# Strassen's scheme for the first feed-forward product of three quarters of an attention, mixing and feed-forward kernel

## The chip, the core and the metric

One core of one Trainium2 chip runs the whole program in one launch. The metric is the device time of the launch in microseconds; lower is better. The engines are TensorE (PE, with its weight loads as PEld), VectorE (DVE), ScalarE (ACT), GpSimd (POOL) and the DMA queues, of which SyncE (SP) issues nearly all. Each engine works through its own list of instructions in order and waits for the others by semaphores.

## What is computed

Three stages follow each other; all arrays are float32 at the end, the large weights arrive as float64 (two 32-bit words each).

```python
# attention, 2 x 8 heads, 768 positions, 64 wide: a local band and 24 block sums
scores_l = scale * q @ k.T           # kept where |i - j| < 16
scores_s = scale * q @ k_sum.T + log(32)
a = softmax(concat([scores_l, scores_s]));  attn = a @ concat([v, v_sum])
# first mixing block, x = attn as (2, 768, 512)
u = x + (x.T @ U @ V).T
x2 = u + relu(u @ w_ch1) @ w_ch2     # w_ch1 512 x 2048, w_ch2 2048 x 512
# second mixing block
xk = mu_k * x2 + (1 - mu_k) * x2_prev;  xr = mu_r * x2 + (1 - mu_r) * x2_prev
out = sigmoid(xr @ w_r) * (relu(xk @ w_k)**2 @ w_v)   # w_k 512 x 1024, w_v 1024 x 512
```

## The kernel before

Every large product is made of three: a number is split into a high part (a copy rounded to the type that TensorE takes, `fp32r`) and a low part (the rest), and high x high, high x low and low x high are added up in PSUM. The high part is made on ACT (`relu_high` L600, `block` L556, `split_high` L739), the low part on DVE or POOL (`relu_low` L605, `block` L560, `split_low` L742, `mix_low` L698).

The order of everything is written out by hand as two lists of steps, `ORDER` (attention, and the first quarter of the feed-forward block for batch 0) and `ORDER2` (the rest). A step is a name and its indices, and calls one function, which issues a few instructions on one or two engines. The list fixes the order on every engine, the SP queue among them.

Of `ORDER2`, in the order of time:

- The feed-forward block. The 2048 hidden columns are four quarters `q` of 512; batch `b` has 768 positions, in two halves `c` of 384. For each (q, b, c) and each of four tiles `i` of 128 hidden columns, `f1` (step `fa`, L595) makes 12 matmuls 128x128 by 128x384 into a bank, `relu_high` (`fh`) and `relu_low` (`fl`) make the two parts of the hidden tile from the bank, and `f2` (`fb`, L618) makes 12 matmuls into four accumulating banks. After four tiles `y_sum` (`fy`, L626) adds the four banks to `y` on DVE. The list alternates `fa` of the next tile with `fb` of this one. `y_rest` (`yr`, L491) adds the low part of `u` to `y` on POOL.
- Weights: 54 blocks of 128x512 float64 are loaded (`cl`) and converted by hand: two ACT steps (`ca` L512, `cb` L515), three DVE steps on SBUF (`cc` L519, `cs` L525, `cg` L529), one POOL addition (`cp` L541); then, for the blocks of `w1`, `w2` and `wr`, the high part on ACT (`ch` L556) and the low part on POOL (`co` L560). They come in the order w1/w2 by quarters, wk, wr, wv; those of wk and wv stay in SBUF (`quads`).
- The product with w_r (`ra`, L707), then `k = xk @ w_k` and the product with w_v, both by Strassen's scheme: seven products (`ka` L772, `va` L804) of sums of quadrants instead of eight of the quadrants. The sums of weights, of `xk` and of the squared hidden values are made by `sums` (L736; `wks`, `xs`, `wvs`, `ms`, with a `p` behind the name on POOL, without it on DVE), split by L739 and L742, and the products are combined from PSUM on DVE (`k_take` L778, `v_take` L816).

`take` and `give` hand out the eight banks of PSUM in turn; SBUF regions are shared by hand (`SLOTS`, `PLACE`).

## Time and profile before

| | us |
|---|---|
| median of 3 runs (498.65 to 501.3) | 500.97 |
| profiled execution | 499.92 |
| its span, first to last instruction | 498.1 |
| PE busy | 484.7 (97%) |
| DVE busy | 401.4 (81%) |
| ACT busy | 276.2 (55%) |
| POOL busy | 252.3 (51%) |

Busy time is the union of an engine's instructions. The span is read in stages: attention and the first half of quarter 0 up to 107.5 us, the second half of quarter 0 up to 141, quarters 1 to 3 up to 341.9, the products with w_r and w_k up to 434, the product with w_v and the output up to 498.1. A row of the view of stages has the engine's busy time in that stage and, in brackets, its instructions. A row of instructions has line, engine, operation, output from input by tile names, shapes, the count, the busy time in us, the mean of one in ns, and the idle time before them with what ended it. Instructions of DVE overlap by some tens of ns, so busy time is a little under the sum of the single ones.

### The profile page before, as it was taken

To read this page: it belongs to the slowest core of one execution; us is meant where nothing else is said; L and a number is where in the kernel's file an instruction comes from. 1 tells how busy PE (TensorE), PEld (TensorE's weight loads), DVE (VectorE), ACT (ScalarE), POOL (GpSimd) and SP (SyncE) were. 2 spreads that over 40 slices of the span, in tenths; PEclk is the share of its full clock that TensorE was granted. 3 is DMA by queue.
4 is the path that set the end of the run, shared out by engine and by line. 5 is a ranking of instruction groups with operands and counts; after the bars stand their busy time and mean duration, and the time that the engine had idled before them with its cause. 6 is when DMAs were issued, how large, how long until landed. Compare 5 with 4: busy or idle time off the path is not lost.

```text
span 498.1 us, 9378 instructions
## 1 busy us (share of the span) xinstructions
PE 484.7 (97%) x3636; PEld 464.1 (93%) x3636; DVE 401.4 (81%) x790; ACT 276.2 (55%) x532; POOL 252.3 (51%) x203
## 2 busy tenths in 40 slices
...
GB/s 312 320 255 216 230 186 50 100 0 170 128 126 138 116 128 168 144 145 135 102 111 1 0 1 1 2 1 84 86 1 1 0 1 1 1 5 60 1 22 169
DMA packets 18061, 46.34 MB, mean 93 GB/s; under 512 B 2897, under 2 KB 7377, under 8 KB 18017
## 3 DMA queue, kind: packets, MB, share of 16 engines
...
q10 hardware_dynamic: 144, 0.18, 0.1%
...
q0 software_dynamic: 32, 0.05, 0.0%
...
## 4 chain that ended last, share of the span: by engine, by line
PE 79%; DVE 10%; ACT 6%; DMA 3%; issue 1%; SPq 0%; DVEq 0%
PE bank L595 24%; PE bank L618 23%; PE bank L772 7%; PE bank L707 7%; PE bank L640 4%; PE bank L663 4%; DMA vt<-vt 3%; PE bank L370 2%; PE bank L415 2%; DVE U L742 2%; PE bank L399 2%; PE bank L804 2%; PE bank L467 1%; DVE N L742 1%; DVE V L742 1%; PE bank L437 1%
## 5 line engine op out<-in xcount | busy, mean ns | idle before, releaser
L541 POOL TENSOR_TENSOR A<-C,A 128x512 int32<-128x512 int32 (+1 forms) x38 | 52.6, 1386 | 50.2 <-DVE C L525 45.0
L605 DVE SCALAR_TENSOR_TENSOR h<-bank,h 128x384 fp32r<-128x384 f32 x56 | 30.9, 552 | 45.0 <-ACT h L600 44.7
L600 ACT ACTIVATE h<-bank 128x384 fp32r<-128x384 f32 x56 | 27.4, 488 | 68.1 <-PE bank L595 68.1
L529 DVE SCALAR_TENSOR_TENSOR A<-stg,A 128x512 int32<-128x512 int32 (+1 forms) x54 | 54.0, 1004 | 6.9 <-ACT A L512 4.8
L512 ACT ACTIVATE A<-stg 128x512 f32<-128x512 uint32 (+1 forms) x54 | 36.4, 673 | 35.5 <-DMA stg<-w 18.6
L519 DVE TENSOR_SCALAR C<-C 128x512 f32<-128x512 f32 (+1 forms) x54 | 43.7, 810 | 3.3 <-POOL A L541 2.0
L525 DVE TENSOR_SCALAR C<-C 128x512 int32<-128x512 int32 (+1 forms) x54 | 41.6, 773 | 0.8
L515 ACT ACTIVATE C<-stg 128x512 f32<-128x512 f32 (+1 forms) x54 | 36.2, 673 | 7.6 <-POOL N L541 5.6
L804 PE MATMUL bank<-N,U 128*128 128x256 f32 x252 | 35.9, 280 | 0.5 <-DVE E L816 0.5
L618 PE MATMUL bank<-h,D 128*128 128x384 f32 x192 | 35.9, 336 | 0.0
L618 PEld LDWEIGHTS bank<-h,D 128*128 128x128 f32 x192 | 33.5, 188 | 0.0
L393 ACT ACTIVATE P<-P,nm 128x120 f32<-128x120 f32 x96 | 29.6, 385 | 6.9 <-DVE nm L382 6.7
L804 PEld LDWEIGHTS bank<-N,U 128*128 128x128 f32 x252 | 32.5, 188 | 0.7 <-issue 0.7
L618 PE MATMUL bank<-h,B 128*128 128x384 f32 x144 | 27.2, 337 | 0.0
L707 PE MATMUL bank<-N,U 128*128 128x512 f32 x108 | 27.1, 395 | 0.0
L618 PEld LDWEIGHTS bank<-h,B 128*128 128x128 f32 x144 | 25.4, 188 | 0.0
L382 DVE CUSTOM_DVE_ANT_0 P<-bank,mask 128x120 f32<-128x120 f32 x96 | 21.0, 277 | 5.3 <-PE bank L370 3.7
L707 PEld LDWEIGHTS bank<-N,U 128*128 128x128 f32 x108 | 20.2, 188 | 4.7
L626 DVE TENSOR_TENSOR Y<-bank,Y 128x384 f32<-128x384 f32 x48 | 23.6, 546 | 1.1 <-PE bank L618 1.0
L698 POOL TENSOR_TENSOR U<-X,U 128x384 fp32r<-128x384 f32 x6 | 7.3, 1208 | 27.6 <-ACT U L695 27.6
L804 PE MATMUL bank<-N,V 128*128 128x256 f32 x144 | 21.0, 282 | 0.0
L541 POOL TENSOR_TENSOR D<-C,A 128x512 int32<-128x512 int32 x8 | 11.8, 1486 | 17.0 <-PE bank L618 10.3
...
## 6 DMA issues: line engine op xcount, KB each, us to landing
...
```

The costliest lines, as they stand in the source:

```text
L512: nc_s.activation(tmp(i, "A"), st[i]["raw"][:, :, 0].bitcast(U32), AF.Copy, scale=2.0 ** -51, bias=2.0)
L515: nc_s.activation(tmp(i, "C"), st[i]["raw"][:, :, 1].bitcast(F32), AF.Abs)
L519: nc_v.tensor_scalar(out=c, in0=c, scalar1=as_float(0x38000000), scalar2=as_float(0x47EFFE00), op0=ALU.max, op1=ALU.min)
L525: nc_v.tensor_scalar(out=c, in0=c, scalar1=3, scalar2=None, op0=ALU.logical_shift_left)
L529: nc_v.scalar_tensor_tensor(out=a, in0=st[i]["raw"][:, :, 1], scalar=-2 ** 31, in1=a, op0=ALU.bitwise_and, op1=ALU.bitwise_or)
L541: nc_p.tensor_tensor(out=to, in0=c, in1=a, op=ALU.add)
L595: nc_t.matmul(held[0][:, 0:CH], w[:, sl], x[:, k], start=(n == 0), stop=(n == 3 * KD - 1))
L605: nc_v.scalar_tensor_tensor(out=hl, in0=held[0][:, 0:CH], scalar=0.0, in1=hh.bitcast(F32), op0=ALU.max, op1=ALU.subtract)
L618: nc_t.matmul(acc_t[q, b, c][d][0][:, 0:CH], w[:, sl], x, start=(i == 0 and n == 0), stop=(i == FT - 1 and n == 2))
L707: nc_t.matmul(held[0], xr(c, i)[:, k, o:o + 128], w, start=(n == 0), stop=(n == 3 * KD - 1))
L772: nc_t.matmul(held[0][:, 0:CH], w[:, sl], x, start=(n == 0), stop=(n == 5))
L804: nc_t.matmul(held[0][:, 0:256], x, w[:, sl], start=(n == 0), stop=(n == 11))
```

## The change

`f1` of the quarters 1, 2 and 3 is replaced by Strassen's scheme. For each (q, b) the matrix of weights (512 x 512) and the input (512 x 768) are cut into four quadrants; `f_prod` (`pa`) makes each of seven products as two tiles `j` of 6 matmuls 128x128 by 128x384. Products 6, 7 and 4 accumulate onto the banks of product 1. `f_copy` copies the banks of product 1 to SBUF on ACT after products 1, 6 and 7 (`pm`, `pc`, `pd`), and `f_add` adds SBUF to the banks of 2, 5 and 3 on DVE (`pb`, `pu`, `pf`, `pg`). `f_high` and `f_low` (`hh`, `hl`) take the hidden tiles from those banks. All seven products of a (q, b) now stand ahead of its eight `fb` steps.

Sums and splits come with it: the sums of weight quadrants (`fs`, DVE, 128x512) and their seven splits (`fwh` ACT, `fwlp` POOL) per quarter, the sums of input quadrants (`xf`, `ts`, DVE, 128x768) and four splits (`th` ACT, `tl` DVE) per batch. For batch 1 `y` is set to high plus low of `u` at the start (`yip`, POOL), and its `yr` steps are gone. The batches go 1, 0, 1, 0, 0, 1.

The blocks of wk, wv and of w1's quarter 1 are converted and stored in DRAM (`park`, step `cd`, on the SP queue) and fetched when they are needed (`wf`, `wq`). Four more blocks are converted in `ORDER` (14, were 10). There are still 54 conversions. Both lists are new; some sums and splits changed between DVE and POOL: of the eight `xs` sums six were on POOL and two on DVE, now two and six; of the four `wks` three were on POOL, now one. Regions moved (`SLOTS`, `PLACE`).

```diff
 ORDER2 = """
-cl10 fa0.1.0.0 fa0.1.0.1 fh0.1.0.0 cl11 ca10 fl0.1.0.0 cb10 cg10 cc10 fb0.1.0.0 cs10 fh0.1.0.1 cp10 fl0.1.0.1
...
+yip1 fa0.1.0.0 yip3 fa0.1.0.1 fh0.1.0.0 fl0.1.0.0 yip0 ts1.3 fb0.1.0.0 fh0.1.0.1 yip2 fa0.1.0.2 fl0.1.0.1
...
+    def y_first(eng, i):
+        eng.tensor_tensor(
+            out=y_part(1, i), in0=u_part(1, i, 0).bitcast(F32), in1=u_part(1, i, 1).bitcast(F32), op=ALU.add
+        )
...
+    def park(nm, o=0, n=KFT):
+        def put(f, w):
+            if (nm, f // 4) not in parked:
+                parked[nm, f // 4] = dram.tile([128, 4, 512], F32, name=f"{nm}{f // 4}")
+            nc.sync.dma_start(out=parked[nm, f // 4][:, f % 4], in_=w)
...
+    def fetch(m, i):
+        nm = ("wk", "wv")[m]
+        h, k = divmod(i, 2)
+        nc.sync.dma_start(
+            out=at(nm, 1024, i).rearrange("p (j c) -> p j c", j=4), in_=parked[nm, h][:, :, 256 * k:256 * k + 256]
+        )
...
     def y_sum(q, b, c, d):
...
-        old = yd if q else u_t[b, c][0][:, d].bitcast(F32)
-        nc_v.tensor_tensor(out=yd, in0=held[0][:, 0:CH], in1=old, op=ALU.add)
+        nc_v.tensor_tensor(out=yd, in0=held[0][:, 0:CH], in1=yd, op=ALU.add)
...
+    def fw_sum(eng, q, j):
+        o, x, y, op = FW_SUMS[j]
+        eng.tensor_tensor(out=fw_part(o), in0=fw_part(x), in1=fw_part(y), op=op)
...
+    def f_prod(q, b, p, j):
+        home = 1 if p in (6, 7, 4) else p
+        if home == p:
+            f_t[p, j] = take()
+        whi, wlo = fw_pair(p)
+        xhi, xlo = fx_pair(b, p)
+        n = 0
+        for k in range(2):
+            sl = slice(256 * j + 128 * k, 256 * j + 128 * (k + 1))
+            for w, x in ((whi, xhi), (whi, xlo), (wlo, xhi)):
+                nc_t.matmul(
+                    f_t[home, j][0][:, 0:CH], w[:, sl], x[:, k], start=(home == p and n == 0), stop=(n == 5),
+                    skip_group_check=(home != p),
+                )
+                n += 1
+
+    def f_copy(to):
+        return lambda q, b, j: nc_s.copy(at(f"{to}{j}"), f_t[1, j][0][:, 0:CH])
+
+    def f_add(p, old, kept):
+        def step(q, b, j):
+            ps, t = f_t[p, j][0][:, 0:CH], at(f"{old}{j}")
+            nc_v.tensor_tensor(out=t if kept else ps, in0=ps, in1=t, op=ALU.add)
...
+    first_blocks += park("w1", FT, FT) + f2_blocks(1) + f1_quads(2) + f2_blocks(2) + wk_blocks[:4] + f1_quads(3)
+    first_blocks += wk_blocks[4:] + f2_blocks(3)
+    first_blocks += [block("wr", k, r32(f"wr{2 * k}"), r32(f"wr{2 * k + 1}")) for k in range(KD)]
+    first_blocks += park("wv")
```

Where the instructions stand, at three places. On PE, quarter 2 and batch 0, before: 12 matmuls of `f1` (L595, input in U, weights in A) between the 12 of `f2` (L618, one hidden tile `h` against one region of weights, three into each of four banks).

```order
L595 MATMUL bank3_2835<-U0_651,A_783 128x384 x12
L618 MATMUL bank6_2723<-h_2825,F_2103 128x384 x3
L618 MATMUL bank7_2724<-h_2825,F_2103 128x384 x3
L618 MATMUL bank0_2725<-h_2825,F_2103 128x384 x3
L618 MATMUL bank4_2726<-h_2825,F_2103 128x384 x3
L595 MATMUL bank2_2872<-U0_651,A_783 128x384 x12
```

The same place in the changed kernel, on PE (L761 is `f_prod`, its inputs in U, A and B, its weights in D, E and F):

```order
L761 MATMUL bank1_3116<-U0_685,D_1990 128x384 x6
L761 MATMUL bank3_3131<-U0_685,D_1990 128x384 x6
L761 MATMUL bank0_3143<-U0_685,D_1990 128x384 x6
L761 MATMUL bank2_3156<-U0_685,D_1990 128x384 x6
L761 MATMUL bank1_3116<-A_882,D_1990 128x384 x6
L761 MATMUL bank3_3131<-A_882,D_1990 128x384 x6
L761 MATMUL bank7_3193<-U1_675,E_2031 128x384 x6
L761 MATMUL bank4_3207<-U1_675,E_2031 128x384 x6
```

The products stand in one row without `f2` between them; the banks 1 and 3 of product 1 come again for product 6 (the fifth and sixth rows).

On DVE at that place, before: conversions (L519, L525, L529), the low part of a hidden tile (L605) after each `f1`, and `y_sum` (L626).

```order
L605 SCALAR_TENSOR_TENSOR h_2825<-bank1_2791,h_2825 128x384
L519 TENSOR_SCALAR C_2827<-C_2827 128x512
L529 SCALAR_TENSOR_TENSOR A_2830<-stg_2808,A_2830 128x512
L525 TENSOR_SCALAR C_2827<-C_2827 128x512
L525 TENSOR_SCALAR C_2788<-C_2788 128x512
L605 SCALAR_TENSOR_TENSOR h_2864<-bank3_2835,h_2864 128x384
L626 TENSOR_TENSOR Y1_1819<-bank6_2723,Y1_1819 128x384
```

And now (L773 is `f_add`, L787 `f_low`, L737 the sum of weight quadrants, L568, L574 and L578 are the conversion):

```order
L773 TENSOR_TENSOR bank0_3143<-bank0_3143,X1_2208 128x384
L574 TENSOR_SCALAR C_3125<-C_3125 128x512
L773 TENSOR_TENSOR bank2_3156<-bank2_3156,X1_2208 128x384
L787 SCALAR_TENSOR_TENSOR B_1183<-bank0_3143,B_1183 128x384
L578 SCALAR_TENSOR_TENSOR A_3167<-stg_3127,A_3167 128x512
L787 SCALAR_TENSOR_TENSOR B_1183<-bank2_3156,B_1183 128x384
L737 TENSOR_TENSOR N1_1956<-N1_1956 128x512
L773 TENSOR_TENSOR X1_2208<-bank4_3207,X1_2208 128x384
L773 TENSOR_TENSOR X1_2208<-bank7_3193,X1_2208 128x384
L737 TENSOR_TENSOR N1_1956<-N1_1956 128x512
```

Additions from PSUM and sums of weights now stand between the low parts and the conversions.

On DVE in the product with w_r, before: the mixing of `x2` (L686), its low part (L698) and two sums of quadrants (L736).

```order
L698 TENSOR_TENSOR U0_651<-X1_3643,U0_651 128x384 x2
L686 SCALAR_TENSOR_TENSOR X1_3643<-Y1_1819,mur_83,X1_3643 128x384 x2
L698 TENSOR_TENSOR U0_651<-X1_3643,U0_651 128x384
L686 SCALAR_TENSOR_TENSOR X1_3643<-Y1_1819,mur_83,X1_3643 128x384
L736 TENSOR_TENSOR V0_3939<-V0_3939,A_3640 128x768
L736 TENSOR_TENSOR A_3640<-A_3640,X2_4127 128x768
```

And now (L849 mixing, L861 low part, L899 sums, L578 a conversion):

```order
L899 TENSOR_TENSOR X2_4135<-V0_4020 128x768
L849 SCALAR_TENSOR_TENSOR N1_1956<-Y1_1866,mur_85,N1_1956 128x384
L899 TENSOR_TENSOR V0_4020<-V0_4020,A_3706 128x768
L578 SCALAR_TENSOR_TENSOR A_3747<-stg_3680,A_3747 128x512
L899 TENSOR_TENSOR A_3706<-A_3706 128x768
L861 TENSOR_TENSOR U1_675<-N1_1956,U1_675 128x384
L899 TENSOR_TENSOR A_3706<-A_3706 128x768
```

Sums that POOL made stand on DVE here, and conversions of wv among them.

## Rows read from the trace of the kernel before

**Rows 1.** The page, busy time of each engine over the span.

```profile
PE 484.7 (97%) x3636; PEld 464.1 (93%) x3636; DVE 401.4 (81%) x790; ACT 276.2 (55%) x532; POOL 252.3 (51%) x203
```

**Rows 2.** The view of stages: stretch, length, busy PE, PEld, DVE, ACT, POOL; clock, DMA.

```profile
0.00:20.00 20.00, 12.54 (x220) 9.78 (x220) 13.80 (x64) 13.04 (x33) 13.65 (x32) 1.00 0.93 320
20.00:107.50 87.50, 86.03 (x1089) 75.18 (x1090) 64.90 (x267) 62.46 (x168) 31.31 (x35) 0.98 0.56 165
107.50:141.00 33.50, 33.50 (x193) 33.50 (x193) 30.71 (x45) 20.60 (x38) 21.47 (x15) 1.00 0.37 126
141.00:341.90 200.90, 200.90 (x1154) 200.90 (x1153) 146.03 (x221) 92.35 (x167) 105.40 (x77) 1.00 0.24 82
341.90:434.00 92.10, 92.10 (x481) 85.54 (x480) 86.18 (x103) 58.48 (x88) 65.85 (x31) 1.00 0.05 18
434.00:498.10 64.10, 59.61 (x506) 59.24 (x504) 59.79 (x97) 29.27 (x41) 14.58 (x16) 1.00 0.15 50
```

**Rows 3.** The chain of work that ended last, in order of time: start, length, what.

```profile
191.29 2.08 PE bank L618 x12
193.37 2.08 PE bank L595 x12
...
358.74 16.80 PE bank L772 x96
...
485.39 8.73 PE bank L804 x72
```

**Rows 4.** Groups of instructions by line and shape, DVE operations that read PSUM.

```profile
L605 DVE SCALAR_TENSOR_TENSOR h<-bank,h 128x384 fp32r<-128x384 f32 x56 | 30.9, 552 | 45.0 <-ACT h L600 44.7
L626 DVE TENSOR_TENSOR Y<-bank,Y 128x384 f32<-128x384 f32 x48 | 23.6, 546 | 1.1 <-PE bank L618 1.0
```

**Rows 5.** The same view, DVE operations on SBUF alone.

```profile
L529 DVE SCALAR_TENSOR_TENSOR A<-stg,A 128x512 int32<-128x512 int32 x53 | 53.4, 1012 | 6.9 <-ACT A L512 4.8 <-POOL D L560 1.2 <-issue 0.6
L519 DVE TENSOR_SCALAR C<-C 128x512 f32<-128x512 f32 x53 | 43.3, 818 | 3.3 <-POOL A L541 2.0 <-ACT C L515 1.2
L525 DVE TENSOR_SCALAR C<-C 128x512 int32<-128x512 int32 x53 | 41.2, 780 | 0.8
L742 DVE TENSOR_TENSOR N<-D,N 128x1024 fp32r<-128x1024 f32 x5 | 6.3, 1258 | 0.0
L789 DVE SCALAR_TENSOR_TENSOR B<-B 128x768 f32<-128x768 f32 x3 | 5.4, 1864 | 0.0
L736 DVE TENSOR_TENSOR A<-A,X 128x768 f32<-128x768 f32 x3 | 2.9, 951 | 0.0
```

**Rows 6.** Instructions in order of time, quarter 2 and after: POOL and DVE side by side.

```profile
248.80 1.68 POOL L541 TENSOR_TENSOR A<-C,A 128x512 int32<-128x512 int32 x1 [0.36 <-DVE C L525]
249.25 1.52 DVE L519 TENSOR_SCALAR C<-C 128x512 f32<-128x512 f32 x1
...
253.24 0.42 DVE L519 TENSOR_SCALAR C<-C 128x512 f32<-128x512 f32 x1
```

**Rows 7.** Groups by line and shape from 341.9 to 434 us, DVE.

```profile
L698 DVE TENSOR_TENSOR U<-X,U 128x384 fp32r<-128x384 f32 x5 | 8.2, 1667 | 0.1
L525 DVE TENSOR_SCALAR C<-C 128x512 int32<-128x512 int32 x5 | 7.4, 1482 | 0.1
...
L529 DVE SCALAR_TENSOR_TENSOR A<-stg,A 128x512 int32<-128x512 int32 x4 | 5.4, 1371 | 0.0
L519 DVE TENSOR_SCALAR C<-C 128x512 f32<-128x512 f32 x4 | 4.8, 1206 | 0.0
```

**Rows 8.** Groups by line and shape over the span, a copy from PSUM on ACT and sums on POOL.

```profile
L784 ACT COPY H<-bank 128x384 f32<-128x384 f32 x6 | 2.8, 480 | 0.1
...
L736 POOL TENSOR_TENSOR X<-V 128x768 f32<-128x768 f32 x2 | 5.6, 2802 | 4.1 <-DVE V L686 4.1
```

**Rows 9.** The view of stages, two shorter stretches: quarter 1, and the product with w_v.

```profile
138.80:172.20 33.40, 33.40 (x193) 33.40 (x192) 30.27 (x40) 16.45 (x30) 24.71 (x20) 1.00 0.34 117
...
440.00:485.40 45.40, 44.90 (x385) 44.73 (x383) 45.19 (x65) 23.36 (x32) 7.29 (x7) 1.00 0.07 24
```

More of the change, by code (lines that the diff above doesn't have):

```diff
@@ L233, in give @@
         free.append(held[1])
+    dram = tc.alloc_tile_pool(name="dram", bufs=1, space=bass.MemoryType.DRAM)
     const = tc.alloc_tile_pool(name="const", bufs=1, side="left")
@@ L562, in block, with r32, first_quarter @@
         return I[nm].bitcast(I32)[f], hi_part, lo_part
-    def quarter_blocks(q, area):
+    def r32(name, n=0, k=0):
+        return lambda: at(name, n, k, F32R)
+    def first_quarter():
         return [
             block(
-                nm, q * FT + i, *(f"{area}{4 * i + 2 * j + k}" for k in range(2)),
-                nc_v if q == 0 and i > 1 and nm == "w1" else nc_p,
+                nm, i, *(r32(f"wa{4 * i + 2 * j + k}") for k in range(2)), nc_v if i > 1 and nm == "w1" else nc_p
             )
@@ L624, in y_sum, with f_xsum @@
         yd = y_t[b][:, d, 1 + c * CH:1 + (c + 1) * CH]
-        old = yd if q else u_t[b, c][0][:, d].bitcast(F32)
-        nc_v.tensor_tensor(out=yd, in0=held[0][:, 0:CH], in1=old, op=ALU.add)
+        nc_v.tensor_tensor(out=yd, in0=held[0][:, 0:CH], in1=yd, op=ALU.add)
+        give(held)
+    XF = {3: (3, 1, ALU.subtract), 1: (1, 0, ALU.subtract), 0: (0, "3", ALU.add), 2: (2, "0", ALU.subtract)}
+    XF_OF = {7: 3, 5: 1, 6: 0, 4: 2}
+    RAW_OF = {1: 0, 2: 2, 3: 3}
+    def f_xsum(eng, b, j):
+        x, y, op = XF[j]
+        whole = (lambda i: y_part(1, i)) if b else xf_part
+        y = xf_part(int(y)) if isinstance(y, str) else whole(y)
+        eng.tensor_tensor(out=xf_part(j), in0=whole(x), in1=y, op=op)
@@ new lines, in fx_pair, with fx_high, fx_low @@
+    def fx_pair(b, p):
+        if p in RAW_OF:
+            return [u_part(b, RAW_OF[p], n) for n in range(2)]
+        return [at(f"t{p}{nm}{b}", dt=F32R).rearrange("p (k c) -> p k c", k=2) for nm in "hl"]
+    def fx_high(b, p):
+        nc_s.copy(fx_pair(b, p)[0], xf_part(XF_OF[p]))
+    def fx_low(eng, b, p):
+        hi, lo = fx_pair(b, p)
+        eng.tensor_tensor(out=lo, in0=xf_part(XF_OF[p]), in1=hi.bitcast(F32), op=ALU.subtract)
+    FW_SUMS = {3: (0, 0, 2, ALU.subtract), 1: (2, 2, 3, ALU.add), 2: (3, 3, 0, ALU.subtract), 4: (1, 1, 3, ALU.subtract)}
@@ L627, in y_sum, with f_low @@
+    def f_low(q, b, c, i):
+        hh, hl = hid[q, b, c, i]
+        held = f_t.pop(f_bank(c, i))
+        nc_v.scalar_tensor_tensor(
+            out=hl, in0=held[0][:, 0:CH], scalar=0.0, in1=hh.bitcast(F32), op0=ALU.max, op1=ALU.subtract
+        )
         give(held)
@@ L886, in build @@
         nc_v.tensor_scalar(out=mu1_t[nm], in0=mu_t[nm], scalar1=-1.0, scalar2=1.0, op0=ALU.mult, op1=ALU.add)
-    for q in range(1, FQ):
-        first_blocks += quarter_blocks(q, ("wa", "wb")[q % 2])
-    first_blocks += quads("wk")
-    first_blocks += [
-        block("wr", k, f"wr{2 * k}", f"wr{2 * k + 1}") for k in range(KD)
-    ]
-    first_blocks += quads("wv")
     def both(name, make):
@@ L899, in build @@
     steps.update({
+        "pa": f_prod, "pm": f_copy("ma"), "pc": f_copy("mb"), "pd": f_copy("ma"), "pb": f_add(2, "ma", 0),
+        "pu": f_add(5, "mb", 1), "pf": f_add(5, "ma", 0), "pg": f_add(3, "mb", 0), "hh": f_high, "hl": f_low,
+        "th": fx_high, "fwh": fw_high, "wq": fetch, "wf": fetch_f1,
         "fa": f1, "fh": relu_high, "fl": relu_low, "fb": f2, "fy": y_sum, "yr": y_rest,
@@ L910, in build @@
     both("rl", mix_low)
+    both("yi", y_first)
+    both("xf", x_first)
+    both("ts", f_xsum)
+    both("tl", fx_low)
+    both("fs", fw_sum)
+    both("fwl", fw_low)
     both("wks", lambda e, j: sums(e, LEFT_SUMS, j, w_part, "wk"))
```

297 lines of the change are left out of this document (177 added, 120 removed), and 19 rows, old and new, of the table PLACE.

## Prediction

> **What bounds the kernel now.** The page comes first: PE is busy for 97% of the span, DVE for 81% [rows 1]. Since a busy PE need not be PE at its peak, the chain of waits is next: there each group of 12 matmuls of `f1` and of `f2` takes 2.08 us and the next group follows on its heels [rows 3]; 96 matmuls of L772 take 16.80 us, 2.10 us per 12 [rows 3]. From 107.5 us to 434 us the view of stages has PE busy for the whole of each stretch at the full clock [rows 2]. So there PE sets the pace, and a matmul of 384 columns costs 2.08 / 12 = 0.173 us. The same view says what stands right behind PE. DVE is busy for 146.0 of 200.9 us in quarters 1 to 3, for 86.2 of 92.1 us (94%) in the products with w_r and w_k, and for 59.8 of 64.1 us in the last product [rows 2]. In a shorter stretch of that last product it is busy for 45.19 of 45.40 us while PE is busy for 44.90 [rows 9]. The kernel is bound by PE, with DVE nearly as full from 342 us on, and the only large idle time of DVE is the 55 us in quarters 1 to 3. That is the room into which this change puts its work.
>
> **What it takes away.** For each (quarter, batch), `f1` was 2 halves x 4 tiles x 12 = 96 matmuls; `f_prod` is 7 products x 2 tiles x 6 = 84 of the same shape. Six such pairs: 72 matmuls fewer, 72 x 0.173 = 12.5 us of PE [rows 3]. All of it lies in the stretch where PE never waits, so it counts in full as long as PE still never waits. Quarters 1 to 3 would need 200.9 - 12.5 = 188.4 us of PE.
>
> **What it adds to ACT and POOL.** Three copies from PSUM for each tile, 36 at 0.48 us [rows 8], are 17 us of ACT, with some splits more. ACT has 92.4 of 200.9 us in these quarters [rows 2], so this is hidden. On POOL the splits of weights take the place of the `yr` steps and of fewer `co` steps; its 105.4 of 200.9 us [rows 2] stay about as they are. Storing and fetching blocks in DRAM goes over the SP queue where DMA is at 0.24 of its time and less [rows 2]. I put all three at nothing. If that cover failed, it would show as waits of the splits on DMA.
>
> **What it adds to DVE in quarters 1 to 3.** Here lies the risk.
> - 48 additions from PSUM (`pb`, `pu`, `pf`, `pg`). The nearest row is `y_sum`, which reads the same bank and the same 384 columns: 0.546 us [rows 4], so 26.2 us. 36 of them write back into PSUM, which no row of before does. Lower bound the same 26 us, since nothing makes them shorter than a `y_sum`; upper bound 0.95 us each, the row of 768 columns [rows 5], 46 us. I take 26.
> - For batch 0, four `xf`, four `ts` and four `tl` of 768 columns: 12 at 0.95 us [rows 5], 11.4 us. (Those of batch 1 lie in quarter 0, where DVE is busy for 30.7 of 33.5 us [rows 2], but seven of eight conversions leave, so they fit.)
> - Eight `fs` of 512 columns, between 0.546 [rows 4] and 0.95 us [rows 5]: 0.68 by the columns, 5.4 us.
> - By the lists, 31 conversions instead of 32 and small changes of splits and mixing, about -3 us together. One conversion is 0.818 + 0.780 + 1.012 = 2.6 us of DVE [rows 5].
>
> Sum: 146.0 + 26.2 + 11.4 + 5.4 - 3 = 186 us of DVE against 188.4 us of PE. DVE goes from 73% to 99%, and its queue is in order: a conversion that waits holds up the low part that `f2` wants. Before, with `f2` of one tile between two `f1`, PE asked for a hidden tile one group later; now the last banks of products 5 and 3 must be added, split and given back before the first `fb` can take its four accumulators, after only some 4 us of products. I charge 2 us of PE waits in the whole stretch, since DVE was held at 45.19 of 45.40 us beside a full PE in the last product [rows 9].
>
> **What it adds to DVE in the products with w_r and w_k.** The lists have eight conversions there instead of four (the blocks of wv come later), so four more: at this stretch's own durations 1.206 + 1.482 + 1.371 = 4.06 us each [rows 7], 16 us; at the mean of the span 2.6 us each [rows 5], 10 us. Four `xs` move from POOL to DVE, 4 x 0.95 = 3.8 us, with one `wks` and one `wkl` of 1.26 us each [rows 5]; two more mixings of 384 columns, at most the 1.67 us of the nearest row each [rows 7], 2 us. Against that two squares go to ACT (2 x 1.86 us [rows 5]), one low part to POOL (1.67 us [rows 7]), and one split of `xk` too (0.95 us [rows 5]). Net +12 to +18 us on 86.2 us. Some comes back, because each sum that leaves POOL is up to 2.8 us [rows 8] in which DVE operations beside it wait; I take +11, a little below the lower end: 97 us, for a stretch in which PE has 92.1 us of work. DVE is the bound there, and PE waits 5 us in all.
>
> **Where a DVE operation waits for POOL.** In the trace the same conversion step takes 0.42 us alone and 1.52 us when a POOL addition started before it: that addition runs from 248.80 for 1.68 us, and the step ends as it does [rows 6]. The mean of 0.818 us [rows 5] is half waiting. Operations that read PSUM do not show it: 0.552 and 0.546 us [rows 4]. The Trainium skill ("SBUF — State Buffer", Who interferes with whom) says that a DVE instruction with two SBUF inputs contends with a GpSimd instruction that reads SBUF, while one with at most one SBUF input, outside the two-port modes, does not; by it the 48 additions stay at their price and every added sum and split can wait. The rows on both kinds agree.
>
> **The other stretches.** The last product keeps its steps but for one gate that moves to POOL: 0. The first 107.5 us have 14 conversions instead of 10, some 4 x 2.6 = 10 us of DVE where it has 78.7 us busy, and 8.9 us in which PE has nothing to do [rows 2], most of it before the first inputs have arrived. The new list loads two blocks of k ahead of the first q. I take 0 with 3 us either way.
>
> **The sum.** Span 498.1 - 12.5 + 2 + 5 = 492.6 us. The profiled execution of before is 1.8 us over its span and the median of the three runs 1.05 us over that, so 495.4: I predict **495 us**.
>
> **The rivals.**
> - *Full gain.* DVE keeps up everywhere, because fewer long POOL sums mean fewer waits. For it: the last product, with DVE full and PE not waiting [rows 9]. Against: 97 us of DVE in 92 us. Time 498.1 - 12.5 = 485.6 in span, 488 us.
> - *The gain is eaten.* The new SBUF operations wait behind POOL as the conversions do. L519 waits 0.818 - 0.42 = 0.4 us on average [rows 5, 6]; for some 20 new sums and splits in quarters 1 to 3 this is 8 us, DVE has 194 us there, and PE waits 6 us more: 498.6 in span, 501 us, no change. This is what the rule above would make of the time, since it lets each of these operations block.
> - *Slower: the DVE queue becomes the bound of the whole middle.* From 141 to 434 us DVE would have 186 + 97 = 283 us to do; before, that stretch took 293 us. If DVE can be busy for less than 283 / 293 = 96.6% of it, because it also waits for PE's products and ACT's copies in turn, the kernel gets slower. With the 93.6% that it reached from 341.9 to 434 us [rows 2] it takes 302.4 us, +9.4: 507.5 in span, 510 us. For it: with PE full in quarter 1 DVE was busy for only 30.27 of 33.40 us [rows 9]. Against: there it had no more to do.
> - *The scheme does not do what it says*, the smaller matmul count being lost to slower matmuls: the L772 products are of this very form and run at 2.10 us per 12 [rows 3]. I give it nothing.
>
> **How the numbers follow.** Forecast, between 489.5 and 498.5 us: 0.34. Full gain, below that: 0.24. Gain eaten, within 0.5% of 501 us: 0.17. Slower by DVE: 0.25. A difference of about 0.5% is what a measurement of this kernel can tell from none. So faster 0.58, same 0.17, slower 0.25. The range leaves out a full gain with 3 us more from attention (below 485) and the far part of the slower case (above 508), about a tenth each.
>
> **What would show it.** In the profile after: PE instructions 144 fewer over PE and PEld together in quarters 1 to 3, that stretch at 188 to 194 us, DVE at 95% or more of it; PE waits that name DVE ahead of the first `f2` group of a pair or ahead of L772; the stretch of w_r and w_k at 95 to 100 us. Attention longer by more than 3 us, PE waiting for splits of weights on POOL, or ACT waiting for fetched blocks would make the prediction wrong by another cause; DVE idle in quarters 1 to 3 with PE waiting beside it would be the slower rival.

## The result and the profile after

The changed kernel takes 505.65 us (median of 6 runs, 503.26 to 509.23) against 500.49 us of the kernel before beside it: ratio 1.0117, 95% interval 1.0073 to 1.0162. It is about 1% slower, where the forecast said 1% faster. Its profiled execution took 506.16 us, with a span of 504.4 us. The medians in this document are of all runs, the ratios of those runs alone that were not in the slower of the machine's two states.

The page of after, busy time of each engine, and the clock that TensorE was granted in 40 slices of the span:

```profile
PE 476.0 (94%) x3564; PEld 454.2 (90%) x3564; DVE 444.5 (88%) x871; ACT 301.0 (60%) x589; POOL 256.6 (51%) x205
...
PEclk9999999996999999999999999999999999999999
```

Beside [rows 1], the 72 matmuls are gone (3636 to 3564) and VectorE has 43 us more to do. What is new is the 6 in the tenth slice. The view of stages of after, with the columns of [rows 2], shows where it lies; I cut the start of the feed-forward block finer than before, and leave out the first 20 us:

```profile
20.00:107.20 87.20, 83.90 (x1084) 73.32 (x1084) 69.48 (x270) 66.64 (x179) 36.10 (x36) 1.00 0.64 180
107.20:112.00 4.80, 4.71 (x28) 4.40 (x26) 1.56 (x4) 2.76 (x6) 0.00 (x0) 1.00 0.41 159
112.00:121.00 9.00, 0.38 (x2) 0.12 (x2) 5.00 (x12) 0.26 (x1) 6.77 (x6) 0.76 0.34 86
121.00:125.00 4.00, 4.00 (x13) 4.00 (x14) 4.00 (x3) 0.83 (x1) 4.00 (x3) 0.50 1.00 329
125.00:150.10 25.10, 25.10 (x141) 25.10 (x140) 20.07 (x24) 11.25 (x21) 19.07 (x14) 0.96 0.19 65
150.10:344.50 194.40, 192.82 (x1096) 191.77 (x1095) 177.47 (x281) 113.74 (x218) 99.40 (x71) 1.00 0.32 103
344.50:434.40 89.90, 89.90 (x469) 83.15 (x468) 87.89 (x116) 59.67 (x92) 57.78 (x29) 1.00 0.24 83
434.40:504.40 70.00, 62.91 (x520) 62.09 (x518) 65.46 (x103) 34.12 (x47) 21.43 (x19) 0.99 0.14 46
```

Attention ends where it did. From the first matmul of `f1` to the first of L870 (the product with w_r, L707 before) the kernel before took 33.5 + 200.9 = 234.4 us [rows 2], the changed one 4.8 + 9.0 + 4.0 + 25.1 + 194.4 = 237.3 us. The saving of 12.5 us was due in just this stretch, so 15.4 us were lost in it. Nine of them are the row from 112 to 121: TensorE is busy for 0.38 us in it. In the next row it works at a granted clock of 0.50, the 1.2 GHz level.

The longest waits of TensorE in after (engine, line, whom it waited for: us in total, times, longest):

```profile
PE bank L697 <- DVE h L684: 8.6, 1, 8.6
...
PE bank L967 <- DVE U L905: 2.3, 2, 1.3
...
PE bank L761 <- ACT X L768: 1.0, 1, 1.0
```

The first one is a single wait of 8.6 us, of `f2` for the first low part of h. Instructions in order of time tell why it came so late. First the DMA issues of SP, in which a row's length includes the time that the queue stood still; then VectorE, with the idle time ahead of a row and its releaser in brackets; then TensorE:

```profile
105.88 0.34 SPq L552 DMA_DIRECT2D stg<-w  x1
107.22 9.84 SPq L640 DMA_DIRECT2D w<-A  x3
117.11 0.43 SPq L1052 DMA_DIRECT2D muk<-moe_mu_k  x1
```

```profile
114.47 1.01 DVE L833 TENSOR_TENSOR Y<-bank,U 128x384 f32<-128x384 f32 x2
119.48 0.82 DVE L1054 TENSOR_SCALAR mu1k<-muk 128x4 f32<-128x4 f32 x1 [4.00 <-DMA muk<-moe_mu_k]
120.22 0.16 DVE L1054 TENSOR_SCALAR mu1r<-mur 128x4 f32<-128x4 f32 x1
120.29 0.54 DVE L684 SCALAR_TENSOR_TENSOR h<-bank,h 128x384 fp32r<-128x384 f32 x1
```

```profile
111.82 0.44 PE L697 MATMUL bank<-h,A 128*128 128x384 f32 x1
120.89 3.89 PE L697 MATMUL bank<-h,A 128*128 128x384 f32 x11 [8.62 <-DVE h L684]
124.58 3.35 PE L674 MATMUL bank<-V,B 128*128 128x384 f32 x12
127.76 2.24 PE L697 MATMUL bank<-h,B 128*128 128x384 f32 x12
```

Read from the top. The new stores of converted w1 (L640) wait on SP for the last conversions of attention's list, and hold the queue from 107.22 to 117.06. The two loads of mu, 2 KB each, which the build issues between its two lists, stand behind them. VectorE had nothing queued ahead of 1 - mu at 115.5, stood there for 4.0 us until mu_k had landed, and the low part of h that TensorE wanted stood behind that. The other half of the 8.6 us lies ahead of 115.5: VectorE first had the late conversions of blocks 10 and 13 to do and, between and behind them, the last operations of attention, all in front of that low part.

After the wait, 23 matmuls take 127.76 - 120.89 = 6.87 us, where they take 23 x 0.173 = 3.98 us at full pace: 2.9 us more at the low clock. So one place costs 8.6 + 2.9 = 11.5 of the 15.4 us.

### The profile page after: what moved, and what is told of

It reads as the page before. It is cut to its first block, busy times and chain, and to the rows that moved or that the text cites. A ratio compares the mean times of both kernels' runs of the same rounds, so it can differ in the third digit from the quotient of the medians.

```text
span 504.4 us, 9466 instructions
## 1 busy us (share of the span) xinstructions
PE 476.0 (94%) x3564; PEld 454.2 (90%) x3564; DVE 444.5 (88%) x871; ACT 301.0 (60%) x589; POOL 256.6 (51%) x205
## 4 chain that ended last, share of the span: by engine, by line
PE 50%; DVE 25%; DMA 10%; ACT 8%; issue 3%; POOL 2%; SPq 0%; DVEq 0%; POOLq 0%; ACTq 0%
PE bank L697 16%; PE bank L761 13%; DMA stg<-w 4%; PE bank L803 4%; PE bank L826 3%; PE bank L870 3%; PE bank L674 3%; DVE U L905 2%; DVE A L578 2%; PE bank L967 2%; PE bank L398 2%; PE bank L443 2%; DVE C L568 2%; DMA vcat<-vw 2%; DVE A L899 2%
## 5 line engine op out<-in xcount | busy, mean ns | idle before, releaser
L578 DVE SCALAR_TENSOR_TENSOR A<-stg,A 128x512 int32<-128x512 int32 (+1 forms) x54 | 46.1, 855 | 6.0 <-ACT A L561 5.9
L568 DVE TENSOR_SCALAR C<-C 128x512 f32<-128x512 f32 (+1 forms) x54 | 37.8, 703 | 5.1 <-ACT C L564 5.0
L574 DVE TENSOR_SCALAR C<-C 128x512 int32<-128x512 int32 (+1 forms) x54 | 34.1, 634 | 1.0
L870 PE MATMUL bank<-P,U 128*128 128x512 f32 x132 | 33.1, 395 | 0.0
L697 PE MATMUL bank<-B,N 128*128 128x384 f32 x168 | 31.7, 340 | 0.6 <-DVE B L787 0.5
L697 PEld LDWEIGHTS bank<-B,N 128*128 128x128 f32 x168 | 29.7, 188 | 1.2 <-DVE B L787 0.7
L870 PEld LDWEIGHTS bank<-P,U 128*128 128x128 f32 x132 | 24.7, 187 | 5.9
L697 PE MATMUL bank<-H,N 128*128 128x384 f32 x144 | 26.1, 339 | 0.0
L697 PEld LDWEIGHTS bank<-H,N 128*128 128x128 f32 x144 | 25.5, 188 | 0.0
L967 PE MATMUL bank<-D,U 128*128 128x256 f32 x144 | 21.3, 282 | 2.3 <-DVE U L905 2.3
L697 PE MATMUL bank<-C,N 128*128 128x384 f32 x120 | 22.8, 339 | 0.0
L773 DVE TENSOR_TENSOR bank<-bank,X 128x384 f32<-128x384 f32 x36 | 19.7, 557 | 3.3 <-ACT X L768 2.5
L697 PEld LDWEIGHTS bank<-C,N 128*128 128x128 f32 x120 | 21.3, 188 | 0.0
```

Source lines behind the costliest of these rows:

```text
L568: nc_v.tensor_scalar(out=c, in0=c, scalar1=as_float(0x38000000), scalar2=as_float(0x47EFFE00), op0=ALU.max, op1=ALU.min)
L574: nc_v.tensor_scalar(out=c, in0=c, scalar1=3, scalar2=None, op0=ALU.logical_shift_left)
L578: nc_v.scalar_tensor_tensor(out=a, in0=st[i]["raw"][:, :, 1], scalar=-2 ** 31, in1=a, op0=ALU.bitwise_and, op1=ALU.bitwise_or)
L697: nc_t.matmul(acc_t[q, b, c][d][0][:, 0:CH], w[:, sl], x, start=(i == 0 and n == 0), stop=(i == FT - 1 and n == 2))
L870: nc_t.matmul(held[0], xr(c, i)[:, k, o:o + 128], w, start=(n == 0), stop=(n == 3 * KD - 1))
L967: nc_t.matmul(held[0][:, 0:256], x, w[:, sl], start=(n == 0), stop=(n == 11))
```

## The experiments

Each kernel was compared with the kernel before on the same chip. "Step" names are those of the lists: `cl` load of a raw block, `ca` to `cg` its conversion on ScalarE and VectorE, `cp` the join on GpSimd, `cd` the store to DRAM; `wf` the fetch of w1; `yi` a sum for Y on GpSimd, `ts` and `fs` the scheme's sums of inputs and of weights on VectorE; `fh`, `fl` copy and low part of h; `fy` the drain of an accumulator. Line numbers shift by a few from kernel to kernel with the edits. Theory Q was that steps which wait stand in an in-order queue ahead of what TensorE needs; the rival D was that VectorE is simply too full.

**Three ways to take the mu wait away.** The first (e1) moves the loads and 1 - mu into attention:

```diff
-cb1 KK2 SPR0 ... E1.0 SPR1 LT3
+cb1 KK2 SPR0 ... E1.0 SPR1 LT3 mm0
-LK4 LQ4 LV2 ... cl2 cg0 cp0 ca1 ...
+LK4 LQ4 LV2 ... cl2 cg0 mo0 cp0 ca1 ...
```

> The changed kernel with the two small loads of mu issued some 75 us earlier and the two small VectorE operations on them (1 - mu) put some 60 us earlier; nothing else moves. Theory Q (the changed kernel loses its gain at one place, 112 to 125 us, where two stores to DRAM hold the SP queue until 117.1, the mu loads stand behind them, and VectorE stands in order at 1 - mu until 119.5): VectorE is then free at 115.5 with the last sums, reaches the first h low part at about 115.5 instead of 120.3, and TensorE's wait of 8.62 us there becomes about 4; with less of the low clock behind it the time is 497 to 501. Rival D (VectorE as a whole is too full and what is gained here is waited for later): 504 to 506, with new waits of TensorE for VectorE between 150 and 430.

Measured: 501.27 us, ratio 1.0014 (0.9982 to 1.0045). TensorE's wait became 3.74 us.

The second (e2) moves the last two stores behind the mu loads:

```diff
-... UL7.1 cp10 Y1.1 Y1.2 cp13 cd10 cd13     (end of ORDER)
+... UL7.1 cp10 Y1.1 Y1.2 cp13
-yip1 fa0.1.0.0 yip3 ...                     (start of ORDER2)
+cd10 cd13 yip1 fa0.1.0.0 yip3 ...
```

> The changed kernel with only the last two stores of converted w1 (of blocks 10 and 13) issued behind the mu loads on the SP queue instead of ahead of them. Theory Q: the mu loads go out at about 107.6 and have landed by 111, VectorE doesn't wait at 1 - mu, TensorE's wait of 8.62 us becomes about 4, 497 to 501 as in the run with mu early. Rival D: 504 to 506. If the mu load itself were the slow thing (many small pieces), the wait at 1 - mu would stay though the stores are gone from ahead of it.

Measured: 500.9 us, ratio 1.0006 (0.9976 to 1.0036). TensorE's wait became 5.0 us. SP in this kernel, in order of time:

```profile
107.23 0.43 SPq L1051 DMA_DIRECT2D muk<-moe_mu_k  x1
...
115.01 1.56 SPq L639 DMA_DIRECT2D w<-A  x2
```

The loads go out ten microseconds earlier, and VectorE comes to 1 - mu at 114.89 and doesn't wait there; the smallness of their pieces was not the cause.

The third (e3) leaves SP as it is and moves only the two VectorE operations:

```diff
-    for nm in "kr":
-        nc_v.tensor_scalar(out=mu1_t[nm], in0=mu_t[nm], ...)
-fy3.0.0.0 ch43 fy3.0.0.3 xa1.0.0.0 ...
+fy3.0.0.0 ch43 fy3.0.0.3 mo0 xa1.0.0.0 ...
```

> The changed kernel with the mu loads where they are, behind the two stores, and only the two VectorE operations on mu put some 200 us later, ahead of their first reader. Theory Q (VectorE's own order passes the wait of the SP queue on to TensorE): the stall shrinks as in the other two, 497 to 501, though the SP queue stays held until 117. Rival: if the held SP queue costs time by what stands behind the mu loads on it (the fetch of w1 and the next raw blocks), the time stays at 503 to 506 while TensorE's wait moves to a later place.

Measured: 500.26 us, ratio 1.0000 (0.9976 to 1.0023). SP is still held, from 106.58 to 116.57, and it no longer matters; TensorE's wait became 3.7 us. The three agree within their intervals: about 5 us, 1%, were the mu wait passed on by VectorE's queue. Theory Q holds for this part; the kernel is now as fast as before, and not faster.

**The same move in the kernel before (e4).**

```diff
-cg1 cp0 LT3 KK3 ... T1.2 K3 GC0 ch1 ...
+cg1 cp0 LT3 mm0 KK3 ... T1.2 K3 mo0 GC0 ch1 ...
```

> The kernel before with the same move of the mu loads and of 1 - mu to an early place. Theory Q: no store stands ahead of the mu loads in the kernel before, VectorE doesn't wait at 1 - mu there (it ran at 110.22 with nothing named), so there is nothing to gain: 498 to 503, ratio 1.00. If the early place were worth something by itself, it would be 495 to 497, as much as the changed kernel gained by it.

Measured: 504.01 us, ratio 1.0076 (1.0051 to 1.01), a miss. I had put 1 - mu too close behind its load, and VectorE stood at it again, this time at 24 us:

```profile
28.59 0.17 DVE L875 TENSOR_SCALAR mu1k<-muk 128x4 f32<-128x4 f32 x1 [4.77 <-DMA muk<-moe_mu_k]
```

TensorE waits 3.78 us there. It is no control of the place, but it shows the same mechanism in the kernel before: a 0.17 us operation that waits for 2 KB costs some 4 us. That the move alone gives nothing in the kernel before was not shown.

**The late conversions behind the low part (e5).** On top of e1:

```diff
-Z1.3.0 U7.1 ca10 cb13 ... cs10 cg13 Y1.0 cg10 UL7.1 cp10 Y1.1 Y1.2 cp13 cd10 cd13
+Z1.3.0 U7.1 UC7.1 UL6.1 Y1.0 UL7.1 Y1.1 Y1.2
-yip1 fa0.1.0.0 yip3 fa0.1.0.1 fh0.1.0.0 fl0.1.0.0 yip0 ts1.3 fb0.1.0.0 ...
+yip1 fa0.1.0.0 yip3 fa0.1.0.1 fh0.1.0.0 fl0.1.0.0 cb13 ca10 cb10 cc13 ca13 cc10 fb0.1.0.0 ...
+cg10 cp10 cp13 cd10 cd13 yip0 ts1.3 yip2
```

> The changed kernel with mu early as in e1, and the last conversions of attention's end (blocks 10 and 13: two copies each on ScalarE, three operations on VectorE, one on GpSimd, the store) moved behind the first low part of h, so that VectorE reaches it as soon as TensorE has the product. Theory Q: the whole stall of 8.62 us and the low clock after it go, the time is 491 to 496, faster than the kernel before. Rival D: no better than e1, since the conversions only come later on a full VectorE, and TensorE waits for the fetched w1 or for VectorE after 125: 498 to 506.

Measured: 499.07 us, ratio 0.9964 (0.9931 to 0.9998), above the 491 to 496 of Q. The wait at the first tile is gone: its low part runs at 109.2 us. A new wait of 4.2 us stands two tiles later. VectorE there:

```profile
118.73 2.54 DVE L715 TENSOR_TENSOR P<-Y 128x768 f32<-128x768 f32 x1 [4.23 <-POOL Y L525]
```

A `ts` waits for GpSimd's sum of Y, which stands behind two joins there, and a low part of h waits behind the `ts`.

**GpSimd's sums first, and four single places later on (e6).** The lists of e5 with `yip0` and `yip2` ahead of the joins, and `ca40`, `wkl1`, `wvs4` and one `ts` each behind a step that TensorE waits for:

> The kernel of e5 with five more places in the lists moved and no work changed: GpSimd's two sums of Y (yip0, yip2) ahead of the two joins of blocks 13 and 10, so that VectorE's sums for Strassen (ts) no longer wait 4.23 us for them with the low part of h behind; that low part ahead of one ts; one ScalarE conversion behind the copy of a product that TensorE waited for at 277 (0.8 us); one low part of w_k behind the low part of h that stood behind it at 326 (0.5 us); one low part of a mixed tile ahead of a sum of w_v at 447 (1.3 us). Theory Q (each loss is one place where a step that waits stands in an in-order queue ahead of what TensorE needs): 489.5 to 493.5. Rival D (VectorE is full, each loss closed opens another): 496 to 500.

Measured: 500.27 us, ratio 0.9993 (0.9967 to 1.002), a miss. The wait for VectorE shrank to 0.5 us, and ScalarE took it over. Waits of TensorE, then ScalarE in order of time:

```profile
PE bank L697 <- ACT h L679: 2.9, 1, 2.9
```

```profile
125.65 0.62 ACT L743 CAST D<-N 128x512 fp32r<-128x512 f32 x1 [2.38 <-DMA N<-w]
```

The copy of a fetched weight waits for the fetch, which waits for the stores, which wait for the joins that I had put later; the copy of h stands behind. So far D foretold more than Q.

**Sparing VectorE (e7, e9).** Whether its load matters is asked directly by leaving the clamp out, on top of e3 (e7):

```diff
         def clamp(i):
+            if i >= 14:
+                return
             c = st[i]["C"]
```

> The kernel of e3 with one VectorE operation of each conversion, the clamp, left out for blocks 14 to 53: 40 operations, 30.9 us of VectorE's time (21.9 of it in the first products' stretch of quarters 1 to 3, 7.5 in the stretch of w_r and w_k), ScalarE, GpSimd and TensorE as they were. Theory Q: in those stretches TensorE waits for VectorE almost nowhere, so the time drops by 0 to 2 us, to 498 to 500.5. Rival D (VectorE bounds these stretches): 480 to 494, since 10 us or more of the 30.9 come back.

Measured: 495.31 us, ratio 0.9909 (0.9883 to 0.9935), where e3 had 1.0000: some 4.5 us come back. VectorE's busy time fell by less than the 30.9 us of the operations left out, from 444.9 to 423.3 us, since others took longer (the mean of VectorE's last conversion step went from 0.876 to 0.931 us, that of `fs` from 1.258 to 1.357). Neither theory foretold that size. From 144 to 425 us no wait of TensorE is left in this kernel's trace. The same cut in the kernel before (e9):

> The kernel before without the clamp of blocks 14 to 53 (the 40 operations that e7 left out). Both theories: TensorE names no wait for VectorE between 141 and 434 in the kernel before, so 0 to 1.5 us, 498.5 to 500.5. If it gains 4 us or more as e7 did, the clamp costs that in either kernel and e7 says nothing of a VectorE made too full by the change; if it gains nothing, what e7 gained is the price of the fuller VectorE.

Measured: 500.71 us, ratio 1.0007 (0.998 to 1.0034). The kernel before gains nothing, though its VectorE is busy for 365.3 us instead of 401.4. So what e7 gains is a price that the change made. That it is VectorE's load alone is not shown: without the clamp each conversion is also one step shorter, and what waits for converted blocks gets them sooner.

**Another order for the first tiles (e8).** The list of e5 with the copies and low parts of h that come next put ahead of `ts` and of the copies of fetched weights:

```diff
-th1.7 ts1.1 fb0.1.0.1 fh0.1.0.2 wf0 ts1.0 yr0.1.0 cl14 fl0.1.0.2 th1.6 ts1.2 fa0.1.0.3 ...
+th1.7 fb0.1.0.1 fh0.1.0.2 wf0 fl0.1.0.2 tl1.7 fa0.1.0.3 yr0.1.0 cl14 wf1 fb0.1.0.2 fh0.1.0.3 fl0.1.0.3 ts1.1
...
```

> The kernel of e5 with only the start of the second list put in another order, no work changed: the steps that TensorE needs next (copies and low parts of h of tiles 2 and 3, and the first of the second half) stand ahead of VectorE's sums for Strassen (which wait for GpSimd's sums of Y) and ahead of ScalarE's copies of the fetched w1 (which wait for the fetch behind the last two stores). Theory Q (the gain of the scheme is all there, and what eats it is a step that waits in an in-order queue ahead of the copies and low parts of h): the wait of 4.2 us at 119 to 123 and the low clock with it go, the span from 495.5 to 489 to 492, the time 490.5 to 494. Rival D (the work on VectorE, GpSimd and ScalarE between 106 and 143 doesn't fit beside the shorter TensorE part, in any order): the wait comes back as one at the first product of the scheme, about 143, and the time stays at 496 to 501.

Measured: 499.99 us, ratio 1.0 (0.997 to 1.0029). TensorE, then VectorE, in order of time:

```profile
127.56 1.75 PE L698 MATMUL bank<-h,A 128*128 128x384 f32 x9
133.06 1.33 PE L698 MATMUL bank<-h,A 128*128 128x384 f32 x3 [3.74 <-DVE Y L705]
```

```profile
129.10 3.44 DVE L738 TENSOR_TENSOR N<-N 128x512 f32<-128x512 f32 x2 [1.20 <-POOL D L748]
132.46 1.47 DVE L705 TENSOR_TENSOR Y<-bank,Y 128x384 f32<-128x384 f32 x3
```

The wait moved again, to 129: now two `fs` stand ahead of the `fy` that frees the accumulators. Ahead of them VectorE waited 1.20 us for GpSimd's low parts of the fetched weights. Is the trip through DRAM what holds it all up? In the next kernel (e10) the stores of w1 are gone and the fetch reads rows of an input:

```diff
         def put(f, w):
+            if nm == "w1":
+                return
...
-                in_=parked["w1", 0][:, 2 * h + i].rearrange(...),
+                in_=I["kt"][2 * h + i][:, 0:512].rearrange(...),
```

> The kernel of e8 with the trip of quarter 1's first weight through DRAM taken apart: the four stores of w1 (blocks 10 to 13) are left out, and the fetch reads rows of an input of the same size that lies in DRAM from the start, so the output isn't the reference's; every computing instruction stays. Theory P (what is left of the loss between 106 and 143 us is this trip: stores at 114 to 118, fetch until 126, and low parts on GpSimd, sums on VectorE and drains of accumulators behind it in order): the wait of 3.7 us at 129 to 133 goes, the scheme's first product starts some 4 us earlier, at 139 to 140, the profiled span is 489 to 492. Rival D (work on VectorE between 106 and 143 is too much by itself): the wait stays within 1.5 us of e8's, 493.5 to 500.

Measured: 500.83 us, ratio 1.0006 (0.9973 to 1.0039). The same wait stands at the same step:

```profile
PE bank L700 <- DVE Y L707: 3.7, 1, 3.7
```

Theory P falls: the trip hides behind other steps that are as late. The fetch is issued at 109.6 us in e10 and at 118.4 in e8, but in both kernels ScalarE's copy of the first fetched weight stands right behind its copy of the last `ts`, which VectorE has ready at 125.7 in e8 and 128.4 in e10. With the clamp left out as well (e11):

> The kernel of e10 (no trip of quarter 1's w1 through DRAM, so its output isn't the reference's) and the clamp of blocks 14 to 53 left out as in e7. If the two causes together are the whole loss, what is left is the 12.5 us that the 72 matmuls are worth: 486 to 490, of which the clamp's part is 3 to 5 against e10. If the scheme's matmuls themselves ran slower than the 0.174 us of the others, 491 to 495 would be left with hardly a wait on TensorE.

Measured: 494.72 us, ratio 0.9889 (0.9834 to 0.9943). The clamp's part is some 6 us here; the wait of 3.7 us at the drain stays.

**The clamp on GpSimd (e12).** GpSimd is busy for half of the span, so I tried to give it 20 of the clamps, on top of e5:

```diff
-            nc_v.tensor_scalar(
+            (nc_p if i >= 14 and i % 2 else nc_v).tensor_scalar(
```

> The kernel of e5 with the clamp of the odd blocks from 15 on (20 operations, some 14 us of VectorE) done on GpSimd instead of VectorE, in the same places of the list. If VectorE's own time is what e7's 5 us came from: 495 to 498, faster than e5. Rival L (a GpSimd operation that reads and writes SBUF holds up VectorE's operations there, as the joins do in the trace of before): what VectorE is spared comes back as waits, 498.5 to 503.

Measured: 516.45 us, ratio 1.0313 (1.0264 to 1.0363), worse than either side said. Groups by line and shape of this kernel (L574 is the conversion step behind the clamp), then a wait of TensorE:

```profile
L568 POOL TENSOR_SCALAR C<-C 128x512 f32<-128x512 f32 x20 | 42.1, 2105 | 4.9 <-ACT C L564 2.9 <-PE bank L761 2.0
...
L568 DVE TENSOR_SCALAR C<-C 128x512 f32<-128x512 f32 (+1 forms) x34 | 27.2, 801 | 0.9 <-ACT C L564 0.9
...
L574 DVE TENSOR_SCALAR C<-C 128x512 int32<-128x512 int32 x53 | 36.0, 684 | 29.8 <-POOL C L568 29.2
```

```profile
PE bank L761 <- ACT X L768: 10.9, 7, 3.2
```

A clamp takes 2.1 us on GpSimd and 0.8 us on VectorE, and VectorE, in order, stood still for 29.2 us in front of the next step until GpSimd had done it. TensorE waited 10.9 us for ScalarE's copies of the scheme's products. That these stood behind conversion steps which had come late is argued from the order of the list. So this run lengthens the conversions and doesn't tell load from length.

**The drains first (e13, e14).** In e8's trace the long wait is for a `fy` that stands behind two `fs`. These go behind the `fy` and the next low part (e13):

```diff
-fa0.1.1.1 ca14 cb14 cb15 fwlp1.2 fwh1.4 ca15 fs1.3 fwlp1.4 fwh1.7 fs1.1 fwlp1.7 fy0.1.0.3 fwh1.5 fy0.1.0.1 ...
+fa0.1.1.1 ca14 cb14 cb15 fwlp1.2 fwh1.4 ca15 fwlp1.4 fy0.1.0.3 fy0.1.0.1
+fy0.1.0.2 fb0.1.1.0 fh0.1.1.1 fy0.1.0.0 fl0.1.1.1 fs1.3 fwh1.7 fwlp1.7 fs1.1 fwh1.5 ...
```

> The kernel of e8 with the four drains of accumulators (fy) and one low part of h put ahead of the first two sums of weights (fs) on VectorE, and what needs these sums on ScalarE and GpSimd behind them; no work changed. In e8 the sums started at 129.1, 1.7 us each beside a low part on GpSimd, and TensorE's last three matmuls of a tile waited 3.7 us for the drain behind them. Theory Q (order alone): that wait goes and none takes its place before the first product of the scheme; that product starts at 139 to 141 instead of 143.4, the profiled span is 488 to 491, the time 490 to 496. Rival D (VectorE, with sums that take twice their time beside GpSimd, has too much to do between 106 and 143 in any order): a wait of 3 us or more comes back before or at the first product, at 142 to 145, and the time stays at 497 to 501.

Measured: 498.54 us, ratio 0.993 (0.9894 to 0.9966): this order is 0.7% faster than the kernel before, and its span of 496.2 us is 8.2 us shorter than the changed kernel's, with the same instructions. From the first `f1` on TensorE runs without a wait to 137.0 and then waits 1.98 us for a low part of h. The time lies in rival D's range and not in Q's; the one long wait is shorter than D's 3 us, and it comes earlier. And with the clamp left out (e14):

> The kernel of e13 and the clamp of blocks 14 to 53 left out on VectorE, as in e7. If the order at the start and VectorE's load behind it are the whole loss, the 12.5 us of the 72 matmuls are all there: 485.5 to 489.5. If the order only moves the wait, 491 to 495.5 as with e7 and e11.

Measured: 492.93 us, ratio 0.9844 (0.9797 to 0.9892), in the range for an order that only moves the wait and not in that for a whole gain. Stages of e13 and, below, of e14: from the first `f1` to 2 or 3 us ahead of the scheme's first product, and from there to L871 or L873, the successors of L870:

```profile
107.20:143.20 36.00, 33.72 (x185) 32.89 (x183) 30.02 (x39) 16.25 (x29) 28.47 (x18) 0.95 0.36 122
143.20:337.50 194.30, 192.58 (x1090) 190.80 (x1091) 179.61 (x281) 112.26 (x216) 100.42 (x73) 1.00 0.32 103
```

```profile
107.70:142.20 34.50, 32.53 (x183) 32.21 (x182) 28.56 (x38) 16.26 (x29) 26.97 (x18) 0.98 0.34 116
142.20:334.70 192.50, 192.50 (x1093) 192.30 (x1093) 160.13 (x250) 112.22 (x216) 101.61 (x74) 1.00 0.33 107
```

From the first `f1` to L707 and its successors: 234.4 us before, 237.3 after, 230.3 in e13, 227.0 in e14. Of the 12.5 us, 4.1 show with the order mended and 7.4 with the clamp left out as well. What still misses in e14 is 3.8 us at one place, a wait of 1.97 us at 137 and a low clock behind it, and about 1.1 us of slower matmuls (below).

Both theories were right for a part. By the ratios, order is worth 1.9% (after to e13, 1.0117 to 0.993; 8.2 us of span), and the clamp 0.9% (e13 to e14; 5.0 us of span).

## Why the prediction was wrong

**The sign.** The saving of 12.5 us was counted rightly, 72 matmuls fewer in a stretch where TensorE didn't wait. The condition that went with it, "as long as PE still never waits", failed at a place that the sum doesn't have.

**The step that failed.** "Storing and fetching blocks in DRAM goes over the SP queue where DMA is at 0.24 of its time and less [rows 2]. I put all three at nothing." The share of DMA time was the wrong row: DMA was not full (0.41 and 0.34 of its time from 107 to 121 us), but the queue that issues it was held for 9.84 us by stores that waited for a join. The sign that I named was waits of the splits on DMA. What waited was a load that the diff doesn't touch, then a VectorE operation that the diff doesn't touch, then TensorE. By e1 to e3 this is 5 us. The other half of the wait of 8.6 us comes from a second term that the sum has at nothing, the four more conversions ahead of 107.5 us: "I take 0 with 3 us either way." Attention did end on time, but two of them, of blocks 10 and 13, were done so late that they stood in front of that same low part (e5).

The Trainium skill ("DMA: Bandwidth & Descriptors", Issuing engines are not separate DMA queues) says that starting DMAs on several engines at once saves only the time on the sequencer to start them, usually small beside the DMA. The issues here of a raw block and of mu_k, which waited for nothing, took 0.34 and 0.43 us, which agrees. What stood for 9.84 us was an issue that waited for a join, and of that the sentence says nothing. Whether the stores on another engine's queue would have done no harm was not tried.

**The sums for batch 1.** The prediction says: "Those of batch 1 lie in quarter 0, where DVE is busy for 30.7 of 33.5 us [rows 2], but seven of eight conversions leave, so they fit." By busy time they do: e13 has VectorE busy for 30.02 of 36.0 us. By order they don't fit easily, since each waits for GpSimd or for a fetch, with a copy, a low part or a drain that TensorE needs behind it. e5, e6 and e8 each closed one such place and found the next; e13 closed e8's, and a wait of 1.98 us was left.

They are also longer than I took. Groups of after by line and shape, on VectorE:

```profile
L773 DVE TENSOR_TENSOR bank<-bank,X 128x384 f32<-128x384 f32 x36 | 19.7, 557 | 3.3 <-ACT X L768 2.5 <-ACT A L561 0.8
L737 DVE TENSOR_TENSOR N<-N 128x512 f32<-128x512 f32 x12 | 14.4, 1197 | 0.1
L715 DVE TENSOR_TENSOR P<-P 128x768 f32<-128x768 f32 x4 | 4.8, 1198 | 0.1
L715 DVE TENSOR_TENSOR P<-Y 128x768 f32<-128x768 f32 x2 | 4.2, 2110 | 0.0
```

An `fs` of 512 columns took 1.20 us where I took 0.68, a `ts` of 768 columns 1.20 to 2.11 where I took 0.95. The additions from PSUM, also those that write back into it, took 0.557 us where I took 0.546: the lower bound was right. The rule of the Trainium skill that the prediction cites ("SBUF — State Buffer", Who interferes with whom) parts these rows rightly, and the rival built on it, at 501 us, was nearer to what e1 to e3 gave (500 to 501) than my forecast. But e1 to e3 reach that time by other waits than that rival names. The row that the prediction took for a VectorE operation held up by GpSimd, the clamp L519, doesn't test the line that the rule draws: it reads one SBUF tile and waits all the same, and whether it runs in a mode that the rule excepts no run shows.

**Quarters 1 to 3.** I foretold 188 to 194 us with VectorE at 95% or more; it was 194.4 with 177.47 us of VectorE, 91%. That 177 lies below my 186 although the sums cost more is luck: a conversion took less, 0.709 + 0.639 + 0.860 = 2.2 us by its means over the span of after instead of 2.6 [rows 5], for 31 of them some 12 us, where I had about -3 for conversions and small changes together. The waits there are 1.5 us (1.0 for ScalarE's copy X, 0.5 for a low part) where I charged 2: right in size. The copy X stood on ScalarE behind the first step of a conversion, which waited for its raw block until 284.5. In e14, without the clamp and with 160 us of VectorE, neither wait is left.

**The products with w_r and w_k, and the last product.** I charged 5 us in the first, for 97 us of VectorE. It was 87.89 us in the row of the stages, TensorE never waited there, and from the first matmul with w_r to the first with w_v it took 92.3 us before and after. I put the last product at 0, and there the loss came. From its own first matmul (2.6 us behind the cut at 434.4 in the stages of after) to the end, before, after, e13 and e14:

```profile
434.10:498.10 64.00, 59.51 (x505) 59.14 (x503) 59.69 (x97) 29.18 (x40) 14.48 (x16) 1.00 0.15 50
437.00:504.40 67.40, 60.31 (x505) 59.49 (x503) 62.86 (x99) 31.58 (x44) 18.82 (x18) 0.99 0.14 48
429.90:496.20 66.30, 60.22 (x505) 59.52 (x503) 61.65 (x99) 30.86 (x43) 17.53 (x17) 0.99 0.15 49
427.00:491.20 64.20, 59.75 (x505) 59.34 (x504) 59.95 (x98) 29.84 (x41) 17.40 (x17) 1.00 0.15 50
```

So after loses 3.4 us there, with 3.2 us more of VectorE; e14 loses 0.2. VectorE, at 98% in the stage ahead, seems to bring arrears into it. That the loss goes with the clamp is shown by e13 and e14 (2.1 us between them); how it is carried is only argued.

**The rivals.** "Slower by the DVE queue" had the right sign and the wrong mechanism: from 150 to 434 us the changed kernel takes 284.3 us, not 302. "The scheme does not do what it says" got nothing. In e14 no wait is named between 142.2 and 334.7, and 1093 matmuls take 192.5 us, 0.1761 us each; before it was 200.9 / 1154 = 0.1741 [rows 2]. But the first of them still run at the low clock behind the wait at 137:

```profile
141.90:143.90 2.00, 2.00 (x8) 2.00 (x8) 2.00 (x3) 0.00 (x0) 2.00 (x2) 0.50 0.61 229
143.90:334.70 190.80, 190.80 (x1088) 190.60 (x1088) 158.44 (x249) 112.22 (x216) 99.91 (x73) 1.00 0.32 105
```

Taken from start to start in the traces, from the first `f1` to L707 and its successors and without the steps of 0.2 us and more (waits and low clock), a matmul takes 0.1744 us before, 0.1752 in after and 0.1753 in e14. That is 0.9 to 1.1 us in all, a small part of the gain that isn't there although nothing is named as waited for. Why stays open.

**The sum by what was measured.** From the first `f1` to L870 in after, by the starts of the matmuls: -12.5, +12.1 (the wait of 8.6 us with its edges and the low clock behind it), +2.4 (the waits in quarters 1 to 3 with theirs), +0.9 (slower matmuls) = +2.9, as by the stages. With nothing in w_r and w_k and +3.4 in the last product this gives the 6.3 us of span.
